# Scores issued ahead of value bursts, a place of its own for one pair's exponentials, and constant matmuls at the start of a fused attention and FFN kernel

## The chip, the cores and the metric

The kernel runs on one core of a Trainium2 chip. The metric is the device time of one execution in microseconds. Each kernel was executed several times, in rounds with the kernel before on the same chip. A run also has a span, from the first to the last instruction in its trace; the time is 1.7 to 1.8 us more than the span.

## The reference, cut to what matters

```python
# q, k, v: 8 batches x 8 heads x 576 x 64; f: 8 x 8 x 576
scores = scale * q @ k.T  +  cum[:, None] - cum[None, :]   # cum = cumsum(log(clip(f)))
attn   = softmax(causal(scores)) @ v
x      = attn, heads side by side, reshaped to 4608 x 512
out    = (sigmoid(x @ w_gate) * (x @ w_val)) @ w_out        # d_ff = 1536
```

## The kernel before

The kernel computes batch 0's attention first ("the first batch": four pairs of heads, with 512 of the 576 tokens as main part). From then on the FFN of one 512-token chunk is interleaved with the attention of later batches, in 36 steps a chunk. A pair's scores come in units U, V and W. One unit is some matmuls into a slot of two PSUM banks, one exponential on ScalarE and one mask on GpSimd. Two slots are used in turn, and each exponential's tile has two buffers. `out_one` gives the sums of the exponentials and, after `yield`, the values: ten matmuls each, "the burst".

```python
    for p in range(HPAIR):
        S_unit(p, "U", p % 2)
        S_unit(p, "V", 1 - p % 2)
        if p + 1 < HPAIR:
            T_step(p + 1, 4, DVEC, ACTC)      # 36 transposes of q and k, two copies
        if p:
            burst = out_one(p - 1, 6, 7)
            next(burst)                       # sums
        S_unit(p, "W", p % 2)
        # ... loads; vg_step(p): v times the gates, on GpSimd for p >= 2
        if p:
            next(burst, None)                 # values
```

In the first FFN chunk, `put(s, ...)` attaches work to a step.

```python
    for w, x, tag in ((7, 0, "D"), (9, 1, "A"), (11, 2, "B")):
        put(w, lambda p=x + 1, tag=tag: S_unit(p, "Z", 1, tag))   # scores of the rest tokens
    put(12, rest_values)                                          # their values (reads the masks)
    # ...
    for x, w in enumerate((5, 9, 12)):
        put(w, lambda x=x: load_w2(x))                            # 512 KB of w_out each, issued by GpSimd
    # out_two at step 18: 120 matmuls of 64 to 384 columns, 2.28 us from first to last in before's
    # trace; the last twelve, of 64, start within 81 ns and take 193 to 201 ns each
```

The softmax here doesn't subtract the row's maximum and nothing guards it: scores larger than these inputs give would overflow.

Of the kernel before, what the change touches and what calls it, by code (L numbers as in the profile page):

```python
# [9 lines left out]
BF16 = mybir.dt.bfloat16  # L10
# [5 lines left out]
def kernel(  # L16
# [11 lines left out]
    nc = tc.nc  # L28
    B, H, S, D = q.shape
    BH = B * H  # L30
    NP = 128
# [3 lines left out]
    HPAIR = H // 2  # L35
# [18 lines left out]
    esb = ctx.enter_context(tc.tile_pool(name="expb", bufs=2))  # L54
# [5 lines left out]
    ps = pp.tile([128, 8, 512], FP32, tag="ps", name="ps")  # L60
# [3 lines left out]
    def single(name, shape, dt):  # L64
        return singles.tile(shape, dt, tag=name, name=name)
# [8 lines left out]
    gv = single("gv", [128, NFT, TCH], BF16)  # L74
    gvx = single("gvx", [128, NFT, TCH // 2], BF16)
# [16 lines left out]
    def load_qk(b, hf, pieces):  # L92
        t = qk_pool.tile([128, NJT * H * D], BF16, tag="io", name="qk_in")
        t = qktiles[b, hf] = t[:, 0:4 * TPP * D].rearrange("p (h c) -> p h c", h=4)
        for h0, h1 in pieces:
            for src, part in ((q, LO), (k, HI)):
                nc.gpsimd.dma_start(  # L97
                    t[part, h0:h1, :],
                    src[b, 4 * hf + h0:4 * hf + h1].rearrange("h (p t) d -> p h (t d)", t=TPP))

    def token_rows(src, b, h0, h1, t):
        n = NP if t < NJT - 1 else TAIL
        return n, src[b, h0:h1, t * NP:t * NP + n, :].rearrange("h p d -> p h d")

    def load_v(b, h0, h1, ts, eng):
        for t in ts:
            n, rows = token_rows(v, b, h0, h1, t)
            eng.dma_start(vbs[b % 2][0:n, t, h0:h1, :], rows)  # L108
# [40 lines left out]
    def load_w1(c0, c1):  # L149
        cs = slice(c0, c1)  # L150
        for src, part in ((moe_w_gate, LO), (moe_w_val, HI)):
            nc.gpsimd.dma_start(w1[part, :, cs], src.rearrange("(s p) c -> p s c", p=64)[:, :, cs])
# [13 lines left out]
    st = {}  # L166
# [5 lines left out]
    def pair_T(p):  # L172
        b, a = divmod(p, HPAIR)
        return qTs[b % 2][:, a, :], kTs[b % 2][:, a * SPAD:(a + 1) * SPAD]


    def k_at(p, jt):
        b, a = divmod(p, HPAIR)
        o = a * SPAD + jt * NP if b < 4 else (jt * HPAIR + a) * NP
        return kTs[b % 2][:, o:o + NP]  # L180
# [5 lines left out]
    def T_step(p, bank, copy_q, copy_k):  # L186
        if bank < 4:
            slot_free(bank // 2)
        b, hf, ho = half_of(p)
        src = qktiles[b, hf]  # L190
        banks = [psh[:, 1024 * x:1024 * x + S] for x in (bank, bank + 1)]
        for t in range(TPP):
            for half, bank in zip((LO, HI), banks):
                for h in range(2):
                    nc.tensor.transpose(  # L195
                        bank[64 * h:64 * h + 64, t * QP:(t + 1) * QP],
                        src[half, ho + h, t * D:(t + 1) * D], ident_bf[half, half])
        qT, kT = pair_T(p)
        for dst, bank, copy in ((qT, banks[0], copy_q), (kT, banks[1], copy_k)):
            copy(dst[:, 0:S].rearrange("p (n t) -> p n t", t=TPP),  # L200
                 bank.rearrange("p (t n) -> p n t", t=TPP))
# [25 lines left out]
    WIDE = {"A": 512, "B": 512, "C": 448, "D": 320}  # L227

    def slot_free(slot):
        while chain and slot in chain_holds[0]:  # L230
            pop_chain()

    def S_unit(p, u, slot, tag=None):
        slot_free(slot)
        sc = 2 * slot
        qT = pair_T(p)[0]
        pieces, w, diag = UNITS[u]
        for jt, i0, i1, c in pieces:
            for h in range(2):
                hp = slice(64 * h, 64 * h + 64)  # L240
                nc.tensor.matmul(ps[:, sc + h, c:c + i1 - i0],  # L241
                                 k_at(p, jt)[hp, :], qT[hp, i0:i1],
                                 start=True, stop=True)
        tag = tag or TAGS.get(u, u)
        e = st[p, u] = esb.tile([128, 2, WIDE[tag]], BF16, tag="e" + tag, name="e" + tag)
        nc.scalar.activation(e[:, :, 0:w], ps[:, sc:sc + 2, 0:w], ACTF.Exp, scale=scale)  # L246
        m, pat = diag(e)
        nc.gpsimd.affine_select(out=m, in_=m, compare_op=ALU.is_ge, fill=0.0,  # L248
                                base=0, pattern=pat, channel_multiplier=-1)

    def vg_step(p, eng=None):
        b, a = divmod(p, HPAIR)
        vg = asb.tile([128, NJT, 2, D + 2], BF16, tag="vg", name="vg")
        st[p, "vg"] = vg
        if p < HPAIR:
            (eng or nc.gpsimd).tensor_copy(vg[:, :, :, D], g_bf[:, :, 2 * p:2 * p + 2])
        (eng or nc.gpsimd).tensor_tensor(  # L257
            out=vg[:, :, :, 0:D], in0=vbs[b % 2][:, :, 2 * a:2 * a + 2, :],
            in1=g_bf[:, :, 2 * p:2 * p + 2].unsqueeze(3).to_broadcast([128, NJT, 2, D]),
            op=ALU.mult)  # L260
# [55 lines left out]
    def out_one(p, bs, bv):  # L316
        pair_region(p, 512 * bs, 0, MAIN, False)
        Z = norm_tile("Z", [128, S])[:, 0:MAIN]
        nc.vector.transpose(Z, ps[:, bs, :])
        r = norm_tile("r", [128, 2, NB])[:, 0, 0:MAIN // 32]  # L320
        inverse(r, Z)
        R = norm_tile("R", [128, 2, S])[:, 0, 0:MAIN]
        spread(R, r)
        yield
        pair_region(p, 512 * bv, 0, MAIN, True)
        scaled(p, 512 * bv, R, 0, MAIN)
        if p == 0:
            cross_x(p, 1, 0, MAIN)
# [196 lines left out]
    make_identity(nc, ident_bf)  # L525
    load_qk(0, 1, ((0, 4),))
    make_identity(nc, ident_f)
    load_v(0, 4, 8, range(NJT), nc.gpsimd)
    load_w1(0, 512)
    for i in range(2):  # L530
# [19 lines left out]
    nc.vector.tensor_copy(g_bf[:, 0:NJT - 1, :], gps[:, 0:NJT - 1, :])  # L550
    nc.vector.tensor_copy(g_bf[0:TAIL, NJT - 1, :], gps[0:TAIL, NJT - 1, :])

    for p in range(HPAIR):
        S_unit(p, "U", p % 2)
        S_unit(p, "V", 1 - p % 2)
        if p + 1 < HPAIR:
            T_step(p + 1, 4, DVEC, ACTC)
        if p:
            burst = out_one(p - 1, 6, 7)
            next(burst)  # L560
        S_unit(p, "W", p % 2)
        if p == 0:
            load_qk(1, 0, ((0, 4),))
            vg_step(0, nc.vector)
            vg_step(1, nc.vector)
        elif p == 1:
            load_w1(512, 1024)
        else:
            vg_step(p)
        if p:  # L570
            next(burst, None)
    load_w1(1024, 1536)
# [140 lines left out]
```

## Time and profile before

| | before |
|---|---|
| time, median of the first three runs | 373.72 us |
| span of the first trace (an execution of 375.15 us) | 373.4 us |
| TensorE busy | 359.3 us, 96% |
| ScalarE, VectorE, GpSimd busy | 52%, 47%, 45% |
| TensorE instructions (matmuls and weight loads) in the trace | 10,523 |

The first trace comes from an execution that was 1.4 us slower than the timed ones. In timelines, the columns are start, duration, engine, line, operation, shapes, count and, in brackets, the idle time of the engine just before with what ended it. A group "x10" is one row.

### The profile page before, as it was taken

What the parts mean: (1) busy time and instruction counts of PE and PEld (TensorE: products, weight loads), DVE (VectorE), ACT (ScalarE), POOL (GpSimd) and SP (SyncE); (2) the same over time, 40 slices, a digit from 0 to 9 for tenths busy, and PEclk for the clock granted to TensorE, in tenths of its full rate; (3) what the DMA queues carried; (4) which work ended last, traced back from release to release, by engine and by line L of the source; (5) the groups of instructions that cost most, each with busy time, mean ns of one, the idle gap of its engine ahead of it and who ended that gap; (6) DMA issues with size and microseconds to landing.
All of it is one profiled execution on the core that took longest, in us unless ns stands there. A gap on an engine that the chain in (4) does not pass through costs nothing.

```text
span 373.4 us, 12210 instructions
## 1 busy us (share of the span) xinstructions
PE 359.3 (96%) x5259; PEld 192.0 (51%) x5264; DVE 176.5 (47%) x382; ACT 195.7 (52%) x294; POOL 168.3 (45%) x265
## 2 busy tenths in 40 slices
PE   2889999999999999999999999999999999999996
PEld 1547545455555545454665566545456544444442
DVE  5775482557375555274708370737064703312320
ACT  5868754574736472848374727471747313323321
POOL 8896745064826663559665946460415000000000
PEclk9999999999999999999999999999999999999999
DMA  8999999599988976789984996596313131011002
GB/s 157 233 209 256 194 182 217 173 213 154 158 164 196 157 84 63 168 182 134 142 185 105 185 177 138 148 159 83 99 59 76 32 102 58 3 56 58 0 24 90
DMA packets 101350, 49.24 MB, mean 132 GB/s; under 512 B 72001, under 2 KB 94401, under 8 KB 101297
## 3 DMA queue, kind: packets, MB, share of 16 engines
q0 software_dynamic: 48704, 20.65, 44.0%
q1 hardware_dynamic: 52448, 27.68, 30.8%
q8 instruction: 41, 0.67, 0.8%
q10 hardware_dynamic: 144, 0.13, 0.1%
q14 instruction: 13, 0.10, 0.1%
HBM read 37.90 MB, written 9.44 MB: 127 GB/s over the span
## 4 chain that ended last, share of the span: by engine, by line
PE 94%; ACT 2%; DMA 1%; issue 1%; DVE 1%; POOL 0%; ACTq 0%; POOLq 0%
PE ps L455 51%; PE ps L495 17%; PE ps L352 8%; PE ps L504 8%; PE ps L241 6%; PE ps L195 2%; PE ps L300 1%; DMA qk_in<-in_k_dram 1%; ACT eC L246 1%; ACT eB L246 0%; ACT eA L246 0%; ACT kT L200 0%; PE ps L417 0%; DVE kT L200 0%; POOL qk_in L97 0%
## 5 line engine op out<-in xcount | busy, mean ns | idle before, releaser
L455 PE MATMUL ps<-xR,w 64*128 64x512 bf16 x1728 | 205.1, 376 | 0.2
L465 DVE SCALAR_TENSOR_TENSOR gv<-sg,ps 128x512 bf16<-128x512 bf16 x108 | 74.0, 686 | 152.2 <-ACT sg L464 149.0
L455 PEld LDWEIGHTS <-w 64*128 64x128 bf16 x1728 | 86.2, 94 | 84.0 <-issue 2.5
L464 ACT ACTIVATE sg<-ps 128x512 bf16<-128x512 f32 x108 | 64.5, 598 | 85.1 <-PE ps L455 83.9
L248 POOL TENSOR_SCALAR_AFFINE_SELECT eC<-eC 128x256 bf16<-128x256 bf16 x32 | 12.9, 404 | 94.4 <-ACT eC L246 94.4
L241 PE MATMUL ps<-qT,kT 64*128 64x320 bf16 (+6 forms) x416 | 47.0, 275 | 2.0 <-ACT kT L200 1.1
L246 ACT ACTIVATE eC<-ps 128x896 bf16<-128x896 f32 (+1 forms) x32 | 28.1, 878 | 20.7 <-PE ps L241 20.4
L257 POOL TENSOR_TENSOR vg<-vb,g_bf 128x640 bf16<-128x640 f32 x30 | 37.8, 1261 | 0.0
L482 ACT ACTIVATE ob<-ps 128x512 f32<-128x512 f32 x35 | 19.6, 596 | 32.2 <-PE ps L504 20.1
L495 PE MATMUL ps<-wox,gvx 64*128 64x512 bf16 x288 | 35.7, 376 | 0.0
L241 PEld LDWEIGHTS <-kT 64*128 64x128 bf16 x416 | 22.9, 96 | 24.0 <-issue 4.9
L246 ACT ACTIVATE eA<-ps 128x896 bf16<-128x896 f32 (+2 forms) x33 | 30.5, 926 | 9.0 <-PE ps L241 8.5
L495 PE MATMUL ps<-wo,gv 64*128 64x512 bf16 x288 | 34.4, 376 | 0.0
L246 ACT ACTIVATE eB<-ps 128x768 bf16<-128x768 f32 (+2 forms) x33 | 27.4, 832 | 10.0 <-PE ps L241 9.2
L504 PE MATMUL ps<-wo,gv 128*128 128x512 bf16 x140 | 32.1, 380 | 0.3 <-issue 0.2
L271 DVE TENSOR_TENSOR xR<-ps,R 128x64 bf16<-128x64 f32 (+2 forms) x68 | 26.2, 429 | 2.1
L108 POOL DMA_DIRECT2D vb<-in_v_dram x30 | 25.2, 849 | 0.2 <-issue 0.2
L263 DVE STREAM_TRANSPOSE R<-r 128x576 f32<-128x576 f32 (+1 forms) x32 | 24.6, 770 | 1.1
L495 PEld LDWEIGHTS <-gvx 64*128 64x128 bf16 x288 | 15.7, 94 | 13.0 <-issue 0.4
L495 PEld LDWEIGHTS <-gv 64*128 64x128 bf16 x288 | 15.3, 94 | 13.7 <-issue 0.5
L246 ACT ACTIVATE eD<-ps 128x640 bf16<-128x640 f32 x30 | 21.1, 702 | 2.0 <-PE ps L241 2.0
L504 PEld LDWEIGHTS <-gv 128*128 128x128 bf16 x144 | 13.4, 98 | 16.7 <-issue 1.4
(82 smaller groups left out, 325.9 us busy)
## 6 DMA issues: line engine op xcount, KB each, us to landing
out_dram<-ob SPq DMA_DIRECT2D x35, 256.0 KB, 2.2
vb<-in_v_dram POOLq DMA_DIRECT2D x20, 256.0 KB, 5.4
xR<-xR SPq DMA_DIRECT2D x20, 144.0 KB, 4.1
gvx<-gv SPq DMA_DIRECT2D x12, 192.0 KB, 4.8
vb<-in_v_dram SPq DMA_DIRECT2D x8, 256.0 KB, 7.3
k_rows<-in_k_dram POOLq DMA_DIRECT2D x16, 128.0 KB, 6.0
q_rows<-in_q_dram POOLq DMA_DIRECT2D x16, 128.0 KB, 5.6
qk_in<-in_q_dram POOLq DMA_DIRECT2D x7, 288.0 KB, 6.7
```

Source lines behind the costliest of these rows:

```text
L108: eng.dma_start(vbs[b % 2][0:n, t, h0:h1, :], rows)
L241: nc.tensor.matmul(ps[:, sc + h, c:c + i1 - i0], k_at(p, jt)[hp, :], qT[hp, i0:i1], start=True, stop=True)
L246: nc.scalar.activation(e[:, :, 0:w], ps[:, sc:sc + 2, 0:w], ACTF.Exp, scale=scale)
L257: (eng or nc.gpsimd).tensor_tensor(out=vg[:, :, :, 0:D], in0=vbs[b % 2][:, :, 2 * a:2 * a + 2, :], in1=g_bf[:, :, 2 * p:2 * p + 2].unsquee ...
L263: nc.vector.transpose(R.rearrange("p (n c) -> p n c", c=32), r.unsqueeze(2).to_broadcast([128, r.shape[1], 32]))
L271: nc.vector.tensor_tensor(out=xR[:, a, r0:r0 + n], in0=psf[:, o + i:o + i + n], in1=R[:, i:i + n], op=ALU.mult)
L352: nc.tensor.matmul(psf[32 * qd:32 * qd + 32, o + a:o + z], lhsT_of(jt, qd), e_of(u, qd)[:, c:c + z - a], start=(y == 0), stop=(y == len(to ...
L455: nc.tensor.matmul(ps[:, bk, :], w1[half, head, ft * NP:(ft + 1) * NP], xR[half, sl, t0:t0 + TCH], start=(first and x == 0), stop=(last an ...
L464: nc.scalar.activation(sg, ps[:, fb, :], ACTF.Tanh, scale=0.5)
L465: nc.vector.scalar_tensor_tensor(out=gv[:, ft, :], in0=sg, scalar=1.0, in1=ps[:, fb + 1, :], op0=ALU.add, op1=ALU.mult)
L495: nc.tensor.matmul(ps[:, bk, :], lhsT, rhs, start=(x == 0 and ft == 0), stop=(x == 1 and ft == NFT - 1))
L504: nc.tensor.matmul(ps[:, 4 + tt, :], gv[:, ft, tt * NP:(tt + 1) * NP], wo[:, ft, :], start=(ft == 0), stop=(ft == NFT - 1))
```

## The change

Its intent: ScalarE should not stand idle while TensorE does a value burst, so the next pair's U goes ahead of the burst. Pair 2's U would then need the buffer that pair 0's values still read, so pair 2's tiles get room in `gv`, which the FFN fills later. Eleven matmuls on constants are to bring TensorE's clock up while it waits for the first loads: in the trace of before, a score matmul of 64x512 takes 604 ns before 17 us and 386 ns from 17.3 us on.

```diff
-        e = st[p, u] = esb.tile([128, 2, WIDE[tag]], BF16, tag="e" + tag, name="e" + tag)
+        if e is None:
+            e = esb.tile([128, 2, WIDE[tag]], BF16, tag="e" + tag, name="e" + tag)
+        st[p, u] = e
...
+    spare = gvx[:, 0:2, :].rearrange("p a c -> p (a c)")
+    nc.vector.memset(spare, 1.0)
+    for _ in range(11):
+        nc.tensor.matmul(ps[:, 3, :], spare[:, 0:NP], spare, start=True, stop=True)
...
+    own = {u: gv[:, 6 + 2 * n:8 + 2 * n, :] for n, u in enumerate("UVW")}
+    def main_unit(p, u, slot):
+        S_unit(p, u, slot, e=own[u] if p == 2 else None)
+    main_unit(0, "U", 0)
     for p in range(HPAIR):
-        S_unit(p, "U", p % 2)
-        S_unit(p, "V", 1 - p % 2)
+        main_unit(p, "V", 1 - p % 2)
...
-        S_unit(p, "W", p % 2)
+        main_unit(p, "W", p % 2)
...
+        if p + 1 < HPAIR:
+            main_unit(p + 1, "U", 1 - p % 2)
...
         if p:
             next(burst, None)
```

More of the change, by code (lines that the diff above doesn't have):

```diff
@@ L231, in slot_free, with S_unit @@
             pop_chain()
-    def S_unit(p, u, slot, tag=None):
+    def S_unit(p, u, slot, tag=None, e=None):
         slot_free(slot)
@@ L560 @@
             next(burst)
-        S_unit(p, "W", p % 2)
+        main_unit(p, "W", p % 2)
         if p == 0:
             load_qk(1, 0, ((0, 4),))
+        elif p == 1:
+            load_w1(512, 1024)
+        if p > 1:
+            vg_step(p)
+        if p + 1 < HPAIR:
+            main_unit(p + 1, "U", 1 - p % 2)
+        if p == 0:
             vg_step(0, nc.vector)
             vg_step(1, nc.vector)
-        elif p == 1:
-            load_w1(512, 1024)
-        else:
-            vg_step(p)
         if p:
```

## The prediction

The sum: 0.65 x 0.83 + 0.35 x 0.55 = 0.73 us, to 373.0 us, taken as 372.9. The 65% are my estimate, and no trace stood behind it. Pair 2's scores start at 16.04 us in before, behind the burst of 14.82. After the views of the matmuls, "them" are the core's 16 DMA engines: the packets of GpSimd's queue took 113.1% of the engines' span.

> **What bounds the kernel now.** I read the page first, then the chain of waits, then the timeline of each engine for the first 45 us, then the groups by shape and the DMA view for the same stretch. The page says where room can be at all:
>
> ```profile
> PE   2889999999999999999999999999999999999996
> POOL 8896745064826663559665946460415000000000
> DMA  8999999599988976789984996596313131011002
> ```
>
> TensorE is at nine tenths or more from the fourth slice (28 us) on, and its row of section 1 has 359.3 us busy of 373.4. So nothing after about 28 us can give much, and the change does not touch it: all its parts lie in the first batch, which ends at about 26 us. GpSimd (POOL) and the DMA engines are also full in the first slices. A gain made in the first batch is kept only if TensorE, which is dense afterwards, finds everything else ready earlier as well.
>
> The chain of waits from 8.9 us to 22.3 us alternates between TensorE (scores L241, sums and values L300, transposes L195) and ScalarE (exponentials L246, kT copies L200). The timeline of ScalarE shows the gaps of that game (columns: start, duration, operation, idle time before with its releaser):
>
> ```profile
> 14.93 0.60 ACT L246 ACTIVATE eC<-ps 128x512 bf16<-128x512 f32 x1 [0.36 <-PE ps L241]
> 16.75 1.02 ACT L246 ACTIVATE eA<-ps 128x1024 bf16<-128x1024 f32 x1 [1.22 <-PE ps L241]
> ```
>
> From 8.93 to 22.19 us ScalarE has 13.26 us, and these two waits and one of 0.20 us at 12.10 are all its real gaps: 1.78 us. TensorE at that time:
>
> ```profile
> 14.50 0.40 PE L241 MATMUL ps<-qT,kT 64*128 64x256 bf16 x2
> 14.82 0.64 PE L300 MATMUL ps<-eA,vg 128*64 128x512 bf16 x2
> 16.04 1.03 PE L241 MATMUL ps<-qT,kT 64*128 64x512 bf16 x8
> 21.62 0.41 PE L300 MATMUL ps<-eA,vg 128*64 128x512 bf16 x2 [0.49 <-DVE Z L319]
> ```
>
> The reader is to see that pair 2's first scores (16.04) stand behind pair 0's value burst (14.82 to 16.04), while ScalarE has nothing to do. The 0.49 us before 21.62 is put down to a VectorE transpose, but GpSimd's own row for pair 2's scaled values ends at 20.30 + 1.26 = 21.56, just before, and these matmuls read them. I take that as the true releaser.
>
> [...] The same score matmul before 17 us, and from 17.3 us on:
>
> ```profile
> L241 PE MATMUL ps<-qT,kT 64*128 64x512 bf16 x6 | 1.8, 604 | 1.2 <-ACT kT L200 1.1
> L241 PE MATMUL ps<-qT,kT 64*128 64x512 bf16 x2 | 0.4, 386 | 0.2 <-DVE r L308 0.2
> ```
>
> 604 ns against 386 ns (the column after busy time is the mean of one). A burst of ten value matmuls takes 1.21 us before and about 0.7 us after. So the slow clock lasts for 17 us here[...]. [...] from 5 to 46 us the GpSimd queue alone fills them.
>
> ```profile
> DMA packets 9171, 9.25 MB, mean 226 GB/s; under 512 B 2159, under 2 KB 8732, under 8 KB 9164
> q0 software_dynamic: 7320, 8.61, 113.1%
> ```
>
> **Part 1, the constant matmuls.** One small memset on VectorE (like the others there, about 0.2 us, at about 1 us, where VectorE later idles 0.97 us for the f load, so free), then eleven 128x512 matmuls into a bank not yet used. At half clock one takes about 0.43 us (estimate: the two concurrent value matmuls of 512 columns hold the next ones off by 15.25 - 14.82 = 0.43). So 11 x 0.43 = 4.7 us, from about 1.3 to 6.0 us. The first real transposes that matter wait for k, at 6.72 us, so the eleven are free. What they buy is the full clock early[...]. I give 65%. If so, the transposes at 6.72 (0.69 us) end some 0.24 us earlier and U of pair 0 is 0.2 us shorter: ScalarE's first exponential moves from 8.93 to about 8.5.
>
> **Part 2, the order.** The order of work on ScalarE is the same before and after (U0 V0 kT1 W0 U1 V1 kT2 W1 U2 ...). Only TensorE's order changes: U of pair p+1 stands ahead of the value burst of pair p-1. The case at 14.50: U2 can follow W1 at once, since slot 0 is free (V1's exponential ended at 14.04). Step by step with the full clock: the W1 scores wait for the sums of pair 0, and these for the mask of W0 on GpSimd, which ends at 13.48 + 0.40 = 13.88 whatever TensorE does, because GpSimd's weight load at 11.29 had waited for a DMA. So sums end at about 14.2, W1's exponential starts at about 14.5 (was 14.93), U2's at 14.5 + 0.52 = 15.0 (was 16.75): 1.7 us earlier. Later exponentials keep that (VectorE's qT copy of pair 3 takes little back), so the last one ends at about 20.5 instead of 22.19. With the slow clock still on: W1 at 14.93, U2 at 15.45, then the transposes of pair 3 and sums of pair 1 again cold, and only about 0.75 us is left at the end.
>
> **Part 3, pair 2's exponentials in gv.** It adds and removes no instruction. With U2 ahead of values 0, pair 2 would need the buffer that pair 0's values still read; its own room makes part 2 possible. gv's second half is first written by the FFN after 40 us. Cost 0.
>
> **What is left at 22 us.** ScalarE's 1.7 us does not reach TensorE whole. GpSimd does masks, weight loads and scaled values in order. From 16.37 its queue is: two weight loads to 17.74, three masks (17.84, 18.75, 19.79) with waits for ScalarE of 0.51 and 0.40 us between them, then the scaled values to 21.56. An earlier ScalarE removes just these 0.91 us and some 0.07 of the last mask's wait, about 0.98 us. So values 2 start at 21.62 - 0.98 = 20.64 us, and TensorE, without gaps from there, is about 1.0 us ahead (0.55 with the slow clock, where the exponential of W2 releases GpSimd later).
>
> **What takes part of it back at 38 us.** GpSimd's timeline:
>
> ```profile
> 33.97 0.76 POOL L155 DMA_DIRECT2D wo<-in_moe_w_out_dram  x1 [2.09 <-DMA w<-in_moe_w_val_dram]
> 36.18 0.76 POOL L155 DMA_DIRECT2D wo<-in_moe_w_out_dram  x1
> 37.25 0.28 POOL L248 TENSOR_SCALAR_AFFINE_SELECT eB<-eB 64x128 bf16<-64x128 bf16 x1 [0.31 <-ACT eB L246]
> 37.92 0.29 POOL L248 TENSOR_SCALAR_AFFINE_SELECT eB<-eB 64x128 bf16<-64x128 bf16 x1 [0.39 <-ACT eB L246]
> ```
>
> The issue at 33.97 waits for a weight load to land, and the DMA queue behind it is full since 5 us, so its time is set by bytes and won't move. After it GpSimd works on to 36.94 without a wait. In the changed kernel the two masks of eB then follow at once: 36.94 + 0.25 + 0.29 = 37.5, not 38.21. The second is the mask of pair 3's rest tokens, which these matmuls read:
>
> ```profile
> 38.38 0.35 PE L417 MATMUL ps<-vg,eB 128*64 128x65 bf16 x10
> ```
>
> They can start at about 37.55: at most 0.83 us earlier. So with the full clock 1.0 shrinks to 0.83 us, and with the slow one 0.55 passes. From there on TensorE is dense, the loads land with room to spare (the w_out pieces 7 us ahead), and the gain is carried to the end.
>
> **Sum.** 0.65 x 0.83 + 0.35 x 0.55 = 0.73 us, to 373.0. I take 372.9, since the scaled values on VectorE may overlap the first mask (0.95 us long where others take 0.43) less, and free GpSimd a little.
>
> **Rivals.** (a) The whole gap of ScalarE arrives at the end: 1.8 to 2.0 us, 371.8. For it: TensorE and ScalarE are the chain from 8.9 to 22 us. Against it: GpSimd's scaled values at 21.56 and its DMA wait at 33.97 lie outside this chain and bound TensorE just behind it. (b) DMA takes everything: a landing that now hides (the first w_gate and w_val pieces, or qk_in of the next batch) becomes the wait, and the time is 373.7. For it: 113% on the queue. Against it: there is no TensorE wait for a DMA after 6.7 us in the list of waits, and the GpSimd wait is only half hidden. (c) The eleven matmuls do not raise the clock, or delay the first transposes: 373.2 for the first; for the second each late 0.43 us would be lost in full, but 0.7 us of room is there. (d) GpSimd slows: the U mask of the next pair now precedes nothing new in its queue, as values carry no GpSimd work, so I give this little.
>
> **Range and chances.** 0.83 is a cap from one engine's timeline, so the middle is 372.9. Rival (a) in part gives the low end, 372.0, and (b) the high end, 373.6. Both are far within 2% (7.5 us): same 0.985, faster 0.01, slower 0.005.
>
> **What would show it right or wrong.** Score matmuls of 64x512 at 386 ns already near 8 us show part 1 right; 604 ns show it wrong. ScalarE's wait before U2's exponential (1.22 us) gone and that one at about 15.0 shows part 2. Values 2 starting near 20.6 directly behind GpSimd's scaled values shows the first cap. GpSimd's w_out issue still near 34.0, and TensorE now waiting before the eB matmuls of L417 near 37.5, shows the second. If that issue moves earlier with the rest, the cap is wrong and rival (a) gains; if TensorE waits for a DMA before 30 us, rival (b) holds.

## The result, and the profile after

The changed kernel takes 375.15 us (375.03 to 375.67, four runs) against 373.75 us of before (373.67 to 374.22, four runs). The ratio is 1.0037, with a 95% interval of 1.002 to 1.0055. Ratios here are the mean time of one kernel's runs over that of the other's of the same rounds, so not quite the ratio of the medians quoted. The change is slower by 1.4 us; I had predicted 0.8 us faster, with a range of 372.0 to 373.6 us.

The two first traces have nearly the same span, 373.3 us after and 373.4 before. Before's was a slow execution of that kernel and after's a fast one, so the spans alone say nothing of the change. What follows reads where each trace wins and loses.

The page of the changed kernel (busy tenths in 40 slices of the span):

```profile
PE   6799989999999999999999999999999999999996
POOL 8995826065836664559665947470515000000000
DMA  8999999599898976699985996695313131011002
```

TensorE is now busy in the first slices too, with constants. Its groups by shape, from 5.9 to 11 us and from 12 to 15.4 us (the number after busy time is the mean of one matmul in ns), then the stretches of the clock (the column between POOL and the DMA share is PEclk, the granted share):

```profile
L241 PE MATMUL ps<-qT,kT 64*128 64x512 bf16 x2 | 0.4, 386 | 0.4 <-DVE kT L200 0.4
...
L241 PE MATMUL ps<-qT,kT 64*128 64x512 bf16 x2 | 0.6, 629 | 0.0
```

```profile
core 0: us, PE busy (x) PEld busy (x) DVE busy (x) ACT busy (x) POOL busy (x), PEclk, DMA share, GB/s
...
5.30:12.00 6.70, 3.98 (x100) 2.28 (x98) 5.19 (x12) 5.73 (x8) 6.23 (x11) 1.00 1.22 231
12.10:15.40 3.30, 3.06 (x54) 1.75 (x54) 1.91 (x5) 2.66 (x5) 3.30 (x7) 0.50 1.15 245
```

Behind the constants the clock is full (granted 1.00 from the first record at 5.20 us, 386 ns at 8 us). It is at half again from 12.03 us for 3.41 us (granted 0.50, 629 ns), though TensorE was busy 3.98 of 6.70 us in between and waited at most 1.16 us at a time. Below, a window is such a time of 3.41 us: the half-clock stretch is one long here, two in w2_late and after_again (6.82 and 6.83 us) and four in after_side (13.65 us). ScalarE and TensorE in the first batch:

```profile
14.63 0.60 ACT L248 ACTIVATE eC<-ps 128x512 bf16<-128x512 f32 x1 [0.64 <-PE ps L241]
15.12 2.18 ACT L248 ACTIVATE gv<-ps 128x1024 bf16<-128x1024 f32 x2
```

```profile
14.19 0.82 PE L241 MATMUL ps<-qT,kT 64*128 64x256 bf16 x4
14.94 0.64 PE L302 MATMUL ps<-eA,vg 128*64 128x512 bf16 x2
...
20.23 0.74 PE L302 MATMUL ps<-gv,vg 128*64 128x512 bf16 x10
```

U of pair 2 stands in the row at 14.19, ahead of the burst at 14.94, and its exponential starts at 15.12 (16.75 before) without a wait. Values 2 start at 20.23 (21.62 before), right behind GpSimd's scaled values, whose row (18.91 and 1.27 us long) ends at 20.18. Then GpSimd and TensorE at the second cap:

```profile
34.59 0.75 POOL L155 DMA_DIRECT2D wo<-in_moe_w_out_dram  x1 [2.79 <-DMA w<-in_moe_w_val_dram]
...
36.80 0.76 POOL L155 DMA_DIRECT2D wo<-in_moe_w_out_dram  x1
37.56 0.55 POOL L250 TENSOR_SCALAR_AFFINE_SELECT eB<-eB 64x128 bf16<-64x128 bf16 x2
```

```profile
38.17 0.22 PE L419 MATMUL ps<-vg,eB 128*64 128x65 bf16 x2 [0.73 <-POOL eB L250]
```

This is the cap I predicted, 0.6 us later than I put it. The DMA queue from 5 to 46 us is as full as before:

```profile
q0 software_dynamic: 7298, 8.60, 113.4%
```

To see how far ahead the changed kernel is, I compare the same VectorE instruction of the FFN's gate in both timelines. Before, and then after:

```profile
34.44 0.69 DVE L465 SCALAR_TENSOR_TENSOR gv<-sg,ps 128x512 bf16<-128x512 bf16 x1 [1.53 <-ACT sg L464]
...
41.71 0.69 DVE L465 SCALAR_TENSOR_TENSOR gv<-sg,ps 128x512 bf16<-128x512 bf16 x1 [1.99 <-ACT sg L464]
```

```profile
33.19 0.69 DVE L467 SCALAR_TENSOR_TENSOR gv<-sg,ps 128x512 bf16<-128x512 bf16 x1 [1.53 <-ACT sg L466]
...
41.32 0.69 DVE L467 SCALAR_TENSOR_TENSOR gv<-sg,ps 128x512 bf16<-128x512 bf16 x1 [2.25 <-ACT sg L466]
```

It is 1.25 us ahead at 34 us and 0.39 us ahead at 41.7 us. At 50 us it is 1.07 us behind. The new loss lies between, in TensorE's timeline, first before and then after:

```profile
47.29 0.22 PE L352 MATMUL ps<-eB,vg 128*32 128x64 bf16 x4
47.44 1.99 PE L455 MATMUL ps<-xR,w 64*128 64x512 bf16 x13
```

```profile
46.80 0.22 PE L354 MATMUL ps<-eA,vg 128*32 128x64 bf16 x4
48.68 0.21 PE L354 MATMUL ps<-eB,vg 128*32 128x64 bf16 x4 [1.66 <-issue]
```

In the changed kernel TensorE stands still for 1.66 us four matmuls before the end of the dense burst of `out_two`, and the view says "issue": it waited for nothing that the profile knows. The FFN's matmuls follow at 48.82 us. In before, the same four matmuls (47.29) follow at once.

The trace has a lead: 41 DMA packets of 16,384 bytes on the queue q8, marked "instruction". TensorE's 10,523 instructions before are 257 for each. From this I estimate that a packet brings TensorE's next 256 instructions (41 x 256 = 10,496); I call these a piece of its program, and the packet's transfer the fetch. I counted TensorE's rows up to the gap, three of its sequencer's among them: it ends at instruction 1472 = 5.75 x 256. (The traces of the last two sets below hold one record more by then, and their count is one higher.) The next 16 KB had started to move at 46.41 us and were in at 47.38 us, and TensorE went on at 48.67 us. The eleven constants with their weight loads are 22 instructions, so instruction 1472 lies 22 instructions, eleven matmuls, earlier in the work than before.

### The profile page after: what moved, and what is told of

Same layout as the page of the kernel before. It is cut to its first block, busy times and chain, and to the rows that moved or that the text cites. A ratio compares the mean times of both kernels' runs of the same rounds, so it can differ in the third digit from the quotient of the medians.

```text
span 373.3 us, 12230 instructions
## 1 busy us (share of the span) xinstructions
PE 361.2 (97%) x5270; PEld 189.2 (51%) x5275; DVE 177.3 (47%) x383; ACT 195.9 (52%) x294; POOL 168.2 (45%) x265
## 4 chain that ended last, share of the span: by engine, by line
PE 88%; DMA 5%; POOL 4%; ACT 1%; issue 1%; DVE 0%; POOLq 0%; ACTq 0%
PE ps L457 48%; PE ps L497 16%; PE ps L506 8%; PE ps L354 8%; PE ps L241 5%; DMA w<-in_moe_w_val_dram 3%; DMA qk_in<-in_k_dram 2%; PE ps L195 1%; POOL qk_in L97 1%; POOL vg L259 1%; PE ps L302 1%; ACT eC L248 0%; POOL wo L155 0%; POOL gv L250 0%; POOL eA L250 0%
## 5 line engine op out<-in xcount | busy, mean ns | idle before, releaser
L457 PEld LDWEIGHTS <-w 64*128 64x128 bf16 x1728 | 85.2, 94 | 84.4 <-issue 1.8
L241 PE MATMUL ps<-qT,kT 64*128 64x320 bf16 (+6 forms) x416 | 44.5, 268 | 2.7 <-ACT kT L200 1.5
L241 PEld LDWEIGHTS <-kT 64*128 64x128 bf16 x416 | 21.3, 94 | 24.2 <-issue 3.6
L248 ACT ACTIVATE eA<-ps 128x896 bf16<-128x896 f32 (+2 forms) x32 | 29.4, 922 | 7.3 <-PE ps L241 6.9
L248 ACT ACTIVATE eB<-ps 128x768 bf16<-128x768 f32 (+2 forms) x32 | 26.4, 827 | 10.0 <-PE ps L241 9.2
L497 PEld LDWEIGHTS <-gv 64*128 64x128 bf16 x288 | 14.2, 94 | 14.8 <-issue 0.8
L354 PEld LDWEIGHTS <-vg 128*32 128x32 bf16 x1120 | 19.9, 97 | 3.1 <-issue 1.8
```

The costliest lines, as they stand in the source:

```text
L241: nc.tensor.matmul(ps[:, sc + h, c:c + i1 - i0], k_at(p, jt)[hp, :], qT[hp, i0:i1], start=True, stop=True)
L248: nc.scalar.activation(e[:, :, 0:w], ps[:, sc:sc + 2, 0:w], ACTF.Exp, scale=scale)
L354: nc.tensor.matmul(psf[32 * qd:32 * qd + 32, o + a:o + z], lhsT_of(jt, qd), e_of(u, qd)[:, c:c + z - a], start=(y == 0), stop=(y == len(to ...
L457: nc.tensor.matmul(ps[:, bk, :], w1[half, head, ft * NP:(ft + 1) * NP], xR[half, sl, t0:t0 + TCH], start=(first and x == 0), stop=(last an ...
L497: nc.tensor.matmul(ps[:, bk, :], lhsT, rhs, start=(x == 0 and ft == 0), stop=(x == 1 and ft == NFT - 1))
```

## The experiments

**Theory 1/2:** the fetch of one 16 KB piece of TensorE's program is late, because the DMA queue is full. Where the piece ends in the work, and when the queue lets the fetch through, decide the loss. **Rivals:** the constants cost through the clock; the new order costs; the trace caught a rare event; the loads alone are what matters. Eighteen more runs were made, in five sets; each set ran on one chip, beside the kernel before.

### Before again

No edit; the kernel before with a new trace.

> The kernel before, unchanged, once more with a trace, since its first trace came from an execution of 375.15 us while its timed runs lie at 373.7. Theory 1 (waits of TensorE for its own instructions, fetched by DMA in 16 KB pieces, decide by tenths of a us and differ from run to run): ratio 1.000 within 0.002, but a span of about 372.0 in this trace, without the two gaps of 0.43 us (near 128 us) and 0.30 us (near 255 us) that the first trace shows. Rival (the first trace is typical and the profile adds a constant): span 373.4 again with the same gaps.

Measured: ratio 0.9985 (0.9966 to 1.0004), which shows how far the same code differs from itself. The span of the trace is 373.3 us, in an execution of 374.99 us, so again not a typical one (median 374.18). The gap near 128 us is gone, the one near 255 us is 0.63 us long. My expectation of 372.0 for this one trace failed; its reason, that such gaps come and go between executions, held. A single span of this kernel is good to about 1 us.

### Constants with next to no activity

```diff
-        nc.tensor.matmul(ps[:, 3, :], spare[:, 0:NP], spare, start=True, stop=True)
+        nc.tensor.matmul(ps[:, 3, 0:16], spare[:, 0:NP], spare[:, 0:16], start=True, stop=True)
```

> The changed kernel with the eleven constant matmuls cut to 16 columns: the same instructions in number, so the 16 KB pieces of TensorE's program begin at the same places, but next to no activity for the clock. Theory 1 (the 1.66 us stall at 47 us is a fetch of instructions that comes late, since TensorE reaches the end of a piece earlier): the stall near 47 us stays at 1 us or more and the time stays at 375 us, ratio about 1.003. Rival (the eleven matmuls cost time through the clock: full clock at 5 us, half again from 12 to 15.4 us): the stall or the loss goes and the time falls to 374 or below.

Measured: 375.78 us, ratio 1.0021 (1.0 to 1.0042); the gap is there, 1.62 us, again at instruction 1472. The clock got full only at 15.07 us. So the gap needs the instructions, not the early clock.

### Without the constants

```diff
-    spare = gvx[:, 0:2, :].rearrange("p a c -> p (a c)")
-    nc.vector.memset(spare, 1.0)
-    for _ in range(11):
-        nc.tensor.matmul(ps[:, 3, :], spare[:, 0:NP], spare, start=True, stop=True)
```

> The changed kernel without the eleven constant matmuls and their memset: 22 instructions fewer on TensorE, so the piece whose lack stalled it ends 11 matmuls later in the work, after the dense burst of small matmuls at 44.8 to 47 us. Theory 1: the stall near 47 us shrinks from 1.66 us to 0.3 to 0.8 us, the one of 0.73 us at 38.2 us stays (it is GpSimd's), and the time falls by 0.6 to 1.3 us against the changed kernel, to 373.8 to 374.5. Rival (the clock): without the early full clock the first batch is slower by about 0.4 us and the time rises above 375.2.

Measured: 374.49 us, ratio 0.9991 (0.997 to 1.0012), 1.3 us less than with the small constants on the same chip. The dense burst ends without a stop, and the FFN's matmuls follow:

```profile
46.76 0.22 PE L354 MATMUL ps<-eB,vg 128*32 128x64 bf16 x4
46.91 2.63 PE L457 MATMUL ps<-xR,w 64*128 64x512 bf16 x19
```

Instruction 1472 now lies eleven matmuls later, among those 19; there one matmul starts at 47.57 us and the next at 48.08 us, 0.50 us apart where 0.21 is usual among them, so 0.29 us is lost and not 1.66. The rest of GpSimd's cap is still there, 0.41 us at 38.1 us.

### The constants alone, in the old order

The same five lines added to the kernel before.

> The kernel before with the eleven constant matmuls alone, the order left as it was. In every trace so far a piece of TensorE's program ends at its instruction 1472, and what follows cannot start before about 48.1 to 48.9 us. Theory 2 (that moment is fixed by when the DMA queue lets the fetch through, and 22 more instructions ahead put it 22 instructions earlier in the work): a gap of 1 us or more ahead of instruction 1472 inside or at the end of the dense burst near 47 us, TensorE about 1 us behind the kernel before at 50 us, and the time 0.8 to 1.2 us above before, ratio 1.002 to 1.003, though the order is the old one. Rival (the order ahead of the value bursts is what costs): no loss, ratio 0.999 to 1.000.

Measured: 375.61 us against 375.13, ratio 1.0013 (0.9997 to 1.003), which is less than I expected and not clear of 1. The mechanism is clear:

```profile
47.08 0.22 PE L352 MATMUL ps<-eA,vg 128*32 128x64 bf16 x4
48.27 0.21 PE L352 MATMUL ps<-eB,vg 128*32 128x64 bf16 x4 [0.97 <-issue]
```

The gap is at the same four matmuls as in the changed kernel, with the old order. The order does not make it.

### Loads of w_out out of the way

```diff
-    for x, w in enumerate((5, 9, 12)):
+    for x, w in enumerate((13, 15, 17)):      # w2_late, in the changed kernel
+    for x, w in enumerate((11, 18, 18)):      # room_after, room_no_const, room_before
```

> The changed kernel with the three loads of w_out put at steps 13, 15 and 17 of the first FFN block instead of 5, 9 and 12, so that GpSimd's masks of the rest tokens no longer stand behind an issue that waits for a landing. Theory 1 (that wait, at 34.59 us, makes the mask of pair 3 late): the 0.73 us wait of TensorE at 38.2 us goes, TensorE is 1.2 us ahead of before at 40 us instead of 0.4. The time may still not fall, as the fetch stall near 47 us takes what comes early: 374.4 to 375.2. Rival (VectorE or ScalarE holds the mask): the wait at 38.2 us stays.

Measured: 375.45 us, ratio 1.0025 (1.0 to 1.005). The wait at 38.2 us is gone and the masks there wait for ScalarE alone, but the trace can't judge theory 1 by it: the clock was at half from 11.23 to 18.05 us in this execution, so TensorE came 1.35 us later to this place (38.00 us against 36.65). The loads now stood ahead of another mask, and TensorE waited 1.01 us for it at 47.0 us. A bad edit, but it gave a clue: with no loads under way from 42.5 to 44 us, the fetch started 0.19 us after TensorE had passed instruction 1216 (= 1472 - 256). In the changed kernel that took 2.76 us.

> The changed kernel with the loads of w_out at steps 11, 18 and 18 of the first FFN block instead of 5, 9 and 12: behind the masks of the rest tokens, and two of them out of the DMA queue at the time of the fetch. Theory 2: the fetch starts within 0.3 us of TensorE passing instruction 1216 (near 44 us) instead of 2.4 us after it, both stalls (0.73 us at 38.2, 1.66 us at 47) go, TensorE is about 1.2 us ahead of before at 50 us, and the time falls from 1.4 us above before to 0.5 to 1.2 us below it, 0.997 to 0.999. Rival (the stall is inherent to the dense burst, not to the DMA queue): the stall of 1 us or more stays near 47 us.

> The same w_out loads at steps 11, 18 and 18, in the changed kernel without the eleven constant matmuls. Theory 2: neither stall, TensorE about 1.0 to 1.3 us ahead of before at 50 us, the time 0.9 to 1.5 us below before, ratio 0.996 to 0.9975, and no worse than with the eleven matmuls. Rival (early clock matters): slower than with the eleven by 0.3 us or more.

> The kernel before with only the w_out loads moved to steps 11, 18 and 18. Theory 2: its own small gap at instruction 1472 (0.4 us near 48.5 us) goes, nothing else changes: 0.2 to 0.5 us below before, ratio 0.9985 to 0.9995. Rival (the move of the loads itself brings the gain of the two other runs, not the order): as much as those, 0.9 us or more below before.

Measured: 378.16, 378.83 and 377.43 us against 375.13; ratios 1.0073 (1.0042 to 1.0104), 1.008 (1.0043 to 1.0118) and 1.0078 (1.0041 to 1.0114). My time was wrong for all three; the fetch came as I had said. In room_after the DMA queue from 43 to 45 us has just this (packets, MB and share of 16 engines):

```profile
DMA packets 3, 0.02 MB, mean 9 GB/s; under 512 B 1, under 2 KB 2, under 8 KB 2
...
q8 instruction: 1, 0.02, 4.3%
q0 software_dynamic: 2, 0.00, 0.4%
```

The fetch starts 0.23 us after instruction 1216, both stalls are gone, and TensorE is 1.34 us ahead of the first trace of before at 50 us, as theory 2 has it. In TensorE's timeline the FFN runs through, and what was lost comes later:

```profile
46.31 2.76 PE L457 MATMUL ps<-xR,w 64*128 64x512 bf16 x24
```

```profile
73.60 1.04 PE L457 MATMUL ps<-xR,w 64*128 64x512 bf16 x4 [2.02 <-DMA xR<-xR]
```

The queue that I emptied at 43 us was needed: two loads of 512 KB and everything behind them came later, up to the crossing of xR, which TensorE awaits at 73 us. The same wait is 2.66 us in room_no_const and 1.75 us in room_before. Behind it the clock was at half for one window in room_after (73.6 to 77.0 us) and in room_no_const (77.3 to 80.7 us). room_no_const, without the constants, lies 0.7 us above room_after, which is the sign of the rival put beside it; but the intervals overlap nearly whole, so these runs don't decide it.

### One load behind the fetch

```diff
+    for x, w in enumerate((11, 11, 18)):      # no constants; one_late
+    put(35, lambda: load_v(2, 0, 8, range(NJT), nc.sync))    # was 26; one_late_v only
```

> No constant matmuls, w_out loads at steps 11, 11 and 18: one load of 512 KB instead of two out of the queue at the time of the fetch. With two the fetch came at once but the later loads shifted by about 2 us and TensorE waited 2 us for the crossed xR at 73 us. Theory 2: the fetch starts by 44.5 us, no gaps at 38 and 47 us, the wait for xR near 72 us 0 to 1 us; net 0.3 below to 0.5 above before in time, ratio 0.999 to 1.0015. Rival (any load moved behind the fetch costs as much later): a wait of 1.5 us or more for xR, ratio 1.004 or more.

> As one_late, with batch 2's v loads at step 35 of the first FFN block instead of 26, behind the crossing of xR on their queue. Theory 2: neither the fetch nor the crossing waits behind other loads; TensorE is 1.0 to 1.3 us ahead of before at 50 us and still at 80 us, and no new wait above 0.3 us comes by 110 us; the time is 0.7 to 1.3 us below before, ratio 0.9965 to 0.998. Rival (the queue has no room at all before 80 us): a new wait of 1 us or more, for values, out stores or the scaled values of batch 2, between 70 and 100 us.

Measured: one_late takes 373.63 us against 374.56, ratio 0.9975 (0.9962 to 0.9989), the best. GpSimd's mask is back to waiting for ScalarE, and the rest tokens' matmuls follow without a gap (those on eA at 37.24 us):

```profile
36.94 0.29 POOL L250 TENSOR_SCALAR_AFFINE_SELECT eB<-eB 64x128 bf16<-64x128 bf16 x1 [0.39 <-ACT eB L248]
37.19 1.52 POOL L155 DMA_DIRECT2D wo<-in_moe_w_out_dram  x2
```

```profile
37.40 0.35 PE L419 MATMUL ps<-vg,eB 128*64 128x65 bf16 x10
```

The fetch started at 44.90 us, TensorE passed instruction 1472 with no gap above 0.21 us, and it waited for no crossing of xR. one_late_v takes 376.75 us, ratio 1.0065 (1.0037 to 1.0092). The rival that I had put beside it holds: the later v loads delay GpSimd's scaled values of batch 2, and TensorE waits 0.68 and 0.98 us for masks at 87 and 89 us.

> The best version again (new order, no constant matmuls, w_out loads at steps 11, 11 and 18). If its gain is real: 0.6 to 1.3 us below before, ratio 0.9965 to 0.9985, no gap at 38 or 47 us. Rival (luck of one chip): ratio 0.999 to 1.001.

> The kernel before with the w_out loads at steps 11, 11 and 18 alone. Theory 2 (order brings about 1 us, and the moved loads let it through; alone they bring only the 0.1 to 0.5 us that before lost at instruction 1472): ratio 0.9985 to 1.000. Rival (the moved loads are the gain): ratio 0.9975 or less, as the version with the new order.

> The changed kernel, constants and all, with the w_out loads at steps 11, 11 and 18. Theory 2: no gap at 38 us; the fetch starts by 45 us and lands near 46, but instruction 1472 lies 11 matmuls earlier, at the end of the dense burst, where TensorE arrives at 46.5 to 47 us, so 0.3 to 0.8 us of gap are left; and the clock, raised at 4 to 7 us, falls back to half for one or two windows until 14 to 18 us, which costs 0 to 1 us from execution to execution. Ratio 0.9985 to 1.001, 0.5 to 1 us above one_late_again. Rival (the constants are harmless once the loads are moved): the same time as one_late_again within 0.3 us.

Measured on another chip, against 374.29 us: 374.07, 374.79 and 375.31 us; ratios 0.9997 (0.9971 to 1.0023), 1.0011 (0.9986 to 1.0037) and 1.0028 (0.9994 to 1.0061). The gain of one_late was not confirmed here: it is clear of 1 on one chip and unclear on the other. Its trace is not free of the loss either: the fetch started at 45.95 us, not 44.90, and at the piece's end two matmuls start 0.45 us apart (0.54 in one_late_v), where I had expected no gap. Its median lies below that of the changed kernel on the first chip, and on the second below that of the changed kernel with the same loads, where the intervals overlap. The moved loads alone show no gain on this chip (one_late_before), but neither does one_late, so which part made the gain on the first chip is not shown. With the constants the gap stays, 0.87 us at the same four matmuls, and the time is 1.2 us above one_late_again, more than the 0.5 to 1 us that I had expected.

### The changed kernel again, and four kernels side by side

> The changed kernel once more with a trace. If the fetch of instructions decides, the large gap ends at instruction 1472 near 47 us again (1.0 to 1.8 us), whatever the clock does in this execution; the clock's half-rate stretches and the small late gaps will lie elsewhere than in the first trace. Ratio 1.002 to 1.004. Rival (the first trace caught a rare event): no such gap, ratio near 1.000.

Measured: 375.62 us against 374.56, ratio 1.0039 (1.0012 to 1.0066). The gap is there again, 0.81 us, at instruction 1472. It is shorter since the fetch was in 0.85 us earlier (46.53 us); TensorE came to instruction 1472 only 0.12 us later, though the clock was at half from 10.25 to 17.08 us in this execution. So the loss was no rare event.

> The changed kernel, on the same chip as the three next to it. Ratio 1.002 to 1.005; the large gap near 47 us ends at instruction 1472.

> Without the constants. If the loss is theirs: ratio 0.9975 to 1.0005, 1 us or more below after_side, no gap above 0.6 us near 48 us. If the order costs: within 0.4 us of after_side.

> Eleven constants of 16 columns. If the 22 instructions carry the loss: within 0.6 us of after_side and 0.6 us or more above no_const_side. If the clock carries it: within 0.4 us of no_const_side.

> 33 constants of 16 columns, 66 instructions. If the pieces are counted in instructions from the start, the gap near 47 us again ends at instruction 1472, which now lies 22 matmuls earlier in the dense burst than with eleven: TensorE arrives some 0.4 us earlier, leaves at the same moment (48 to 48.8 us) and has 22 small matmuls of 18 ns left to do after it, so a gap of 1.2 to 2.2 us and 0.3 to 0.5 us more loss than tiny_side at 50 us. Rival (the gap belongs to a place in the work, not to a count): the gap stays at the same matmuls as with eleven.

| on one chip, before 374.65 us | time, us | ratio (95%) | full clock in the trace, us | gap at the piece's end |
|---|---|---|---|---|
| no constants (no_const_side) | 374.30 | 0.9990 (0.9958 to 1.0022) | from 17.24 | 0.70 us, in the FFN's matmuls |
| 11 of 16 columns (tiny_side) | 374.98 | 1.0006 (0.9979 to 1.0034) | from 15.57 | 1.19 us, in the dense burst |
| 33 of 16 columns (tiny_33) | 374.41 | 0.9991 (0.9965 to 1.0016) | from 17.34 | none |
| 11 of 512 columns (after_side) | 375.83 | 1.0028 (0.9998 to 1.0058) | 6.86 to 10.28, again from 23.93 | 0.29 us |

The gap column is the time between TensorE's last instruction before and its first after the end of the piece, so it is 0.2 to 0.4 us more than the idle time that a timeline shows after the last matmul has ended.

tiny_33 was a miss: I expected the gap earlier in the burst and more loss. The gap did not stay at the same matmuls either, as the rival has it: there was none. With 66 instructions more, TensorE passes instruction 1216 at 42.78 us, the fetch starts at 44.99 us and is in before the end of the piece is reached. So more instructions were not more loss here (0.9991 against 1.0006 of tiny_side); I read it as a race between the end of a piece and its fetch, which can be won by chance.

after_side shows what else can cost. The trace by stretches, and TensorE's longest wait in the half-clock stretch:

```profile
7.00:10.20 3.20, 2.14 (x85) 1.56 (x85) 1.23 (x4) 1.91 (x4) 3.15 (x6) 1.00 1.21 207
10.40:23.90 13.50, 10.03 (x142) 5.54 (x140) 9.04 (x15) 8.74 (x12) 8.88 (x17) 0.50 1.22 224
```

```profile
17.42 0.61 PE L241 MATMUL ps<-qT,kT 64*128 64x512 bf16 x2 [1.91 <-DVE qT L200]
```

The clock was full at 6.86 us, lost at 10.28 us and back at 23.93 us, four windows of 3.41 us later. A late v load held VectorE for 2.89 us until 14.18 us, its qT copy came late, and U of pair 2, now ahead of the burst, made TensorE wait for that copy. In the traces of the other three kernels on this chip VectorE waits at most 0.46 us for that load, so here the cost of the clock and that of a late load can't be told apart. The trace was of the slowest of the six executions (378.01 us). Each of the changed kernel's 16 executions comes with its mean granted clock, in which one half-clock window counts 0.5 x 3.41 / 374 = 0.0046. Sorted by that clock, with the windows estimated from it (the three traces among them have one, two and four):

| mean clock | half-clock windows after the early full clock | executions | mean span, us |
|---|---|---|---|
| 0.989 to 0.995 | one or two | 10 | 373.5 |
| 0.985, 0.986 | three | 4 | 374.2 |
| 0.981, 0.982 | four | 2 | 376.4 |

In before, and in the kernels without real constants, the clock record starts, at full, between 14.69 and 19.50 us in the traces (17.08 us in before's, where score matmuls of 64x512 took 602 to 606 ns until then and 386 ns after), and only room_no_const falls back to half, at 77.3 us. These executions have no clock record ahead of that, so the same table can't be made for them.

### The fetch in numbers

These times are read from the trace's DMA records of the instruction queue and from TensorE's rows. "Passes 1216" is when the instruction after TensorE's first 1216 starts; "gap" is the time between the starts of two successive instructions at the piece's end.

| kernel | passes 1216, us | fetch starts | fetch in | gap | goes on |
|---|---|---|---|---|---|
| before | 44.92 | 46.13 | 47.02 | 0.50 | 48.60 |
| after | 43.65 | 46.41 | 47.38 | 1.85 | 48.67 |
| after_again | 43.76 | 45.55 | 46.53 | 1.00 | 47.94 |
| tiny_const | 43.56 | 46.28 | 47.22 | 1.81 | 48.55 |
| const_only | 43.93 | 45.86 | 46.84 | 1.17 | 48.27 |
| no_const | 44.40 | 45.46 | 46.47 | 0.50 | 48.08 |
| one_late | 43.95 | 44.90 | 45.93 | none | |
| room_after | 42.97 | 43.21 | 44.59 | none | |
| room_before | 45.63 | 45.78 | 46.84 | none | |

Where TensorE waited, it went on 1.3 to 1.6 us after the fetch was in. Where the DMA queue was empty (the last two rows, and room_no_const with 45.63 and 45.60 us), the fetch started within 0.25 us of instruction 1216; where it was full, 1.0 to 2.8 us after. That is the evidence for the cause: for this piece the delay follows the state of the queue, and the place follows the count. It does not make instruction 1216 a mark for every piece: over the 40 piece ends in each of the first traces of before and after, the fetch starts from 1.9 us ahead of the instruction 256 before the end to 4.6 us after it. Among the FFN's matmuls (before, no_const) 0.21 us of a gap is the usual distance of two starts.

The same traces hold more of it than this one piece, which the experiments were not made for. After 26 us, 24 waits of TensorE of more than 0.25 us are named "issue" in the 20 traces, and every one stands at the end of a piece, counted on from 1472 in steps of 256: at 1472, 3520, 4288, 7104 or 8128, within three records. TensorE went on 1.29 to 1.80 us after that piece was in, and at none of the 800 piece ends in the traces sooner than 1.23 us after. The constants bring a second loss of this kind: at instruction 7104, near 220 us, TensorE waits 0.27 to 1.11 us in seven of the nine traces with eleven constants, and in none of the others. In after_again:

```profile
220.18 0.60 PE L497 MATMUL ps<-wo,gv 64*128 64x512 bf16 x4 [1.11 <-issue]
```

Before's first trace waits 0.43 and 0.30 us in this way at 128 and 254 us, after's first trace not at all there. Before was 1.07 us ahead at 50 us and 0.1 us behind at the end; these two waits are 0.73 of the 1.2 us between.

## Why the prediction was wrong

**The step that failed** is the end of "What takes part of it back at 38 us": "From there on TensorE is dense, the loads land with room to spare (the w_out pieces 7 us ahead), and the gain is carried to the end." My list lacked one load, that of TensorE's own program; by the table above I take it as the one that TensorE waited for, 1.66 us at 47 us. The gain of 0.39 us that reached 41.7 us met the fetch at 46.8 us and became a loss of about 1 us. Before had been up against the same fetch: it goes on at 48.60 us, after at 48.67 us. In the six rows of the table with the loads where they were, the fetch starts at 45.46 to 46.41 us and no earlier for the kernels that pass instruction 1216 a microsecond sooner, so being early gained nothing, and the 22 instructions made TensorE stop eleven matmuls earlier in the work. Four of these are at the tail of the burst and seven are FFN matmuls, which take 0.97 us in the chain of waits of before. The chain of waits of before, which I read before I predicted, has 0.13 us of "issue" at 48.48 us: this fetch. I took such rows for missing records. Not each of them is a fetch: 0.25 us of "issue" at 24.42 us stands at instruction 541, which is no piece's end.

**"so the eleven are free"** (part 1) failed with it. They were free where I looked, ahead of 6.7 us: they ran from 1.53 to 5.87 us, though the memset took 0.48 us and not 0.2. On the one chip with all variants, the 22 instructions cost 0.0016 (1.0006 less 0.9990, 0.6 us) and the early clock, with after_side's late load in it, 0.0022 (1.0028 less 1.0006, 0.8 us); on the first chip the instructions cost 0.0030 (1.0021 less 0.9991, 1.1 us). The intervals of the single ratios are about 0.003 wide to each side, so the split is a likely one and not a settled one. In the new order the constants as a whole cost 1.2 to 1.8 us by three pairs of ratios: 0.9990 and 1.0028 here, 0.9997 and 1.0028 with the w_out loads moved (one_late_again, one_late_const), and 0.9991 and 1.0037 to 1.0039 in earlier sets. In the old order const_only has 0.5 us, not clear of 0, and the two room runs show no cost.

**The clock.** I gave 65% to the full clock coming early and holding. It came (386 ns at 8 us), and it did not hold: it was lost at 10 to 12 us in every trace with real constants, for one to four windows. The doubt had too little weight. That an execution with more half-clock windows is slower is shown by the 16 executions. Whether the early full clock makes the later half clock longer than it would have been is not shown, since the others have no record there.

**Part 2, the order,** was right in each step that I named: U2's exponential at 15.12 us (I said 15.0), values 2 at 20.23 us directly behind GpSimd's scaled values (20.6). But I read the gain off against one trace whose clock came at 17.08 us. In one_late_before, with the old order and the full clock from 14.69 us, the FFN's gates are 0.94 us ahead of that trace at 29 us with no change of the first batch at all. In no_const, with the new order and the full clock from 15.30 us, they are 1.01 us ahead. My estimate from these traces is that at like clock the order is worth some tenths of a microsecond here. In time the runs show 0.1%, not clear of 0: 0.9991 and 0.9990, with intervals that hold 1.

**Part 3** was right: the room in gv adds nothing and nothing waits for it.

**The cap at 38 us** was right in kind and mis-sized. The issue that waits for the landing came at 34.59 us where I had put 33.97, so the masks ended at 38.11 us (I said 37.5), and TensorE was left 0.39 us ahead instead of 0.83.

**The rivals.** Rival (b), DMA takes everything, was nearest, but for another transfer than those I had named. Rival (c) named the constants, with too small a loss. I looked for a wait of TensorE for a DMA before 30 us as its sign; the wait came at 47 us, under the name "issue".

**The base.** I set my time against the timed 373.72 us, and took all durations from a trace of an execution that had needed 375.15 us.

**What stays open.** Why TensorE goes on only 1.3 to 1.8 us after its instructions are in; how the 1.4 us divide between the fetches and the clock; what exactly makes the clock fall back at 10 to 12 us; and whether one_late beats before by 0.9 us, as on one chip, or not at all, as on the other.

## What to carry to other kernels

Count what a change adds to the busiest engine's instruction stream (22 instructions here), and place each gap named "issue" by its instruction count. In these traces all 24 such gaps of more than 0.25 us after 26 us stood within three records of 1472 or of a multiple of 256 after it, and TensorE went on 1.29 to 1.80 us after a packet of the instruction queue was in; the 22 instructions put the first of these places eleven matmuls earlier in the work. With the DMA queue full (113% from 5 to 46 us), the changed kernel was 0.39 us ahead at 41.7 us and 1.07 us behind at 50 us, and moving two loads of 512 KB out of the way of the fetch made TensorE wait 2.02 us for xR at 73 us; so ask for each load which wait it ends next. Look also at how long the clock that warm-up matmuls bring is kept: here it was gone after one or two windows of 3.41 us in every trace with real constants. Whether work that follows without pauses keeps it was not tested.
